# One tile per column piece of w_in, a later gate for the inputs, and a new order table

## The chip, the cores and the metric

The kernel runs on one core of one Trainium2 chip. The time is the device time of one execution in microseconds (us); the spans, waits and durations below come from one profiled execution of the kernel before the change.

## The reference

A gated linear recurrence over 768 time steps, for 4 batches and 8 heads of 48 features, gives x; a two-layer network with a leaky ReLU follows.

```python
f = 1.0 / (1.0 + np.exp(-f_logit))
for t in range(S):
    state = f[:, :, t, :, None] * state + np.einsum('bhd,bhe->bhde', k[:, :, t], v[:, :, t])
    y[:, :, t] = np.einsum('bhd,bhde->bhe', q[:, :, t], state)
x = y.transpose(0, 2, 1, 3).reshape(B * S, H * D)      # 3072 x 384
h = x @ w_in                                           # 384 x 2048
out = np.maximum(0.01 * h, h) @ w_out                  # 2048 x 384
```

## The kernel before

The time axis is cut into 6 chunks of 128 steps, and the 4 batches into 2 groups of 2. A chunk and a group make a "pair", numbered 0 to 11, and a pair has two units (batches) 0 and 1. A unit's attention is a chain over several engines:

- four loads of 192 KB each (`Lf`, `Lk`, `Lq`, `Lv`, line 98, all issued by SyncE, the engine SP);
- `gate` (two ACT instructions on f, lines 136 and 137), `cs` (TensorE sums the logs along time, lines 142 and 145), `dec` (ACT exponentials, lines 152 to 156);
- `q` and `k` (the scaling of q and k on VectorE or GpSimd, lines 167 and 161), `v` (GpSimd casts v, lines 174 and 175);
- `tq`, `tk` (transposes on TensorE, line 188), `cq`, `ck` (VectorE copies them out, line 191), `sc` (scores, line 207), `mk` (VectorE masks, line 212), `mx` (TensorE, line 240), `xt` (VectorE copies the result, x transposed, out, line 246);
- `pt`, `sf`, `sb`: the state for the next chunk (TensorE line 251, VectorE lines 256 and 257, GpSimd lines 261 and 264).

The two-layer network follows for each unit. For pairs 0 to 3 it goes unit by unit: `uu_j_a_g` (line 289) is one of four groups of 12 matmuls against a quarter of the columns of w_in, `pu` the ReLU of it on ACT (line 294). From pair 4 on, `up_j_g` (line 276) takes both units in eight groups of 6 wider matmuls, and `pr` is its ReLU (line 282). `dn_j_a_n` (line 299) is a quarter of the product with w_out, 4 matmuls; `ob` copies the result out (line 304) and `st` stores it (line 312).

The weights are cast to bf16 on the way in, by seven DMAs that GpSimd issues (`W_0` to `W_6`): w_in in three column pieces (line 111; the first and the second a quarter of the columns each, the third a half), then w_out in four pieces (line 115). All three pieces of w_in lie in one tile, `w_in_b`, 128 partitions x 3 x 2048. Group g of `uu` reads columns 512g to 512g+511, in each of the 3 slices: groups 0 and 1 read pieces 0 and 1, groups 2 and 3 read piece 2.

`hold` (`H_n`, line 128) is a tiny DMA issued by SP that reads an element of piece n of the weights, so that SP waits there until this piece has landed; what follows in SP's queue, the loads of pair 2 and later, is issued after that.

Every engine takes its instructions in the order in which a table of words, written out in the kernel, records them: `W_0_3_1_0` is a weight piece, `uu_0_1_2` the group 2 of pair 0, unit 1. Waits between engines are set by the recording layer from the tiles that instructions read and write.

Of the kernel before, what the change touches and what calls it, by code (L numbers as in the profile page):

```python
# [15 lines left out]
def kernel(  # L16
# [60 lines left out]
    w_in_b = const.tile([128, NK, FF], BF16, tag="w_in")  # L77
# [24 lines left out]
    w_in_cols = ((0, FF // 4), (FF // 4, FF // 2), (FF // 2, FF))  # L102

    def weights(piece, x, j, a):

        if (x, j, a) not in seen:
            seen.add((x, j, a))
            nc.gpsimd.tensor_copy(out=gate_w[:, 0:1], in_=raw(j, "fkqv"[x])[0:1, a, H - 1, D - 1:D])
        if piece < 3:
            lo, hi = w_in_cols[piece]  # L110
            nc.gpsimd.dma_start(out=w_in_b[:, :, lo:hi], in_=moe_w_in[:, lo:hi].rearrange("(k p) n -> p k n", p=128))  # L111
        else:
            n = NF // 4
            part = piece - 3
            nc.gpsimd.dma_start(
                out=w_out_b[:, part * n:(part + 1) * n, :],
                in_=moe_w_out[part * n * 128:(part + 1) * n * 128, :].rearrange("(p a) n -> p a n", a=n))
# [3 lines left out]
    def hold(piece):  # L121

        if piece < 3:
            hi = w_in_cols[piece][1]
            src = w_in_b[0:1, NK - 1, hi - 4:hi]
        else:
            src = w_out_b[0:1, (piece - 2) * (NF // 4) - 1, 0:4]
        nc.sync.dma_start(out=gate_s[:, 0:4], in_=src)
# [137 lines left out]
    def columns(ff):  # L266

        c, a = divmod(ff, 4)
        return slice(512 * c + a, 512 * c + 512, 4)

    def up(j, g):
        pm = st[j]["pm", g] = ps_m.tile([128, 2, 256], FP32, name="pm", tag="pm")
        for i in range(2):
            ff = 2 * g + i
            for kk in range(NK):
                nc.tensor.matmul(pm[:, i, :], w_in_b[:, kk, columns(ff)],  # L276
# [7 lines left out]
    def up_unit(j, a, g):  # L284
        pm = st[j]["pu", a, g] = ps_m.tile([128, 4, 128], FP32, name="pm", tag="pm")
        for i in range(4):
            ff = 4 * g + i
            for kk in range(NK):
                nc.tensor.matmul(pm[:, i, :], w_in_b[:, kk, columns(ff)], st[j]["xT"][:, kk, a, :],  # L289
# [58 lines left out]
    Lf_0_0 Lk_0_0 Lq_0_0 Lv_0_0 Lf_0_1 gate_0_0 Lk_0_1 Lq_0_1 cs_0_0 dec_0_0 Lv_0_1 v_0_0 Lf_1_0 q_0_0 k_0_0 tq_0_0  # L348
    gate_0_1 Lk_1_0 cq_0_0 Lq_1_0 cs_0_1 tk_0_0 dec_0_1 Lv_1_0 pt_0_0 ck_0_0 sf_0_0 v_0_1 Lf_1_1 sc_0_0 q_0_1 gate_1_0
    Lk_1_1 k_0_1 tq_0_1 mk_0_0_0 Lq_1_1 tk_0_1 mk_0_0_1 cs_1_0 Lv_1_1 cq_0_1 pt_0_1 dec_1_0 ck_0_1 mx_0_0 W_0_3_1_0  # L350
    sf_0_1 sc_0_1 W_1_3_1_0 xt_0_0 gate_1_1 W_2_3_1_0 mk_0_1_1 q_1_0 cs_1_1 W_3_3_1_0 dec_1_1 v_1_0 mk_0_1_0 tq_1_0
    k_1_0 v_1_1 q_1_1 tk_1_0 mx_0_1 cq_1_0 tq_1_1 sb_0_0 ck_1_0 xt_0_1 sc_1_0 k_1_1 W_4_3_1_0 W_5_3_1_0 cq_1_1 tk_1_1
    uu_0_0_0 mk_1_0_1 W_6_3_1_0 ck_1_1 uu_0_1_0 pu_0_0_0 mk_1_0_0 pu_0_1_0 sc_1_1 mx_1_0 uu_0_0_1 xt_1_0 uu_0_1_1
    mk_1_1_0 pu_0_0_1 mk_1_1_1 pt_1_0 pu_0_1_1 uu_1_0_0 mx_1_1 pu_1_0_0 uu_1_0_1 xt_1_1 pu_1_0_1 uu_0_0_2 uu_0_1_2
    pu_0_0_2 pt_1_1 pu_0_1_2 uu_0_1_3 uu_0_0_3 pu_0_1_3 dn_0_0_0 pu_0_0_3 uu_1_0_2 H_4 Lf_2_0 dn_0_1_0 pu_1_0_2 Lk_2_0
    uu_1_1_0 Lq_2_0 dn_0_1_1 dn_0_0_1 uu_1_0_3 dn_0_0_2 Lv_2_0 pu_1_0_3 dn_0_1_2 pu_1_1_0 Lf_2_1 dn_0_0_3 uu_1_1_1
    gate_2_0 Lk_2_1 ob_0_0 dn_0_1_3 sf_1_0 pu_1_1_1 st_0_0 uu_1_1_2 ob_0_1 cs_2_0 sf_1_1 Lq_2_1 dn_1_0_0 dec_2_0
    dn_1_1_0 v_2_0 st_0_1 uu_1_1_3 k_2_0 sb_0_1 Lv_2_1 gate_2_1 q_2_0 tk_2_0 dn_1_0_1 ck_2_0 Lf_3_0 pu_1_1_2 tq_2_0
    pt_2_0 dn_1_1_1 cq_2_0 pu_1_1_3 Lk_3_0 sf_2_0 sc_2_0 cs_2_1 Lq_3_0 mk_2_0_0 dn_1_1_2 dec_2_1 mk_2_0_1 dn_1_0_2
    Lv_3_0 mx_2_0 k_2_1 v_2_1 Lf_3_1 dn_1_0_3 xt_2_0 sb_1_0 tk_2_1 q_2_1 gate_3_0 Lk_3_1 uu_2_0_0 ck_2_1 tq_2_1  # L360
    pu_2_0_0 cs_3_0 Lq_3_1 cq_2_1 uu_2_0_1 dec_3_0 ob_1_0 sc_2_1 Lv_3_1 uu_2_0_2 mk_2_1_0 pu_2_0_1 q_3_0 st_1_0
    dn_2_0_0 k_3_0 pu_2_0_2 sb_2_0 pt_2_1 mk_2_1_1 gate_3_1 tq_3_0 Lf_4_0 tk_3_0 dn_1_1_3 sf_2_1 v_3_0 dn_2_0_1 Lk_4_0
    ck_3_0 cq_3_0 cs_3_1 sb_1_1 Lq_4_0 mx_2_1 dec_3_1 sc_3_0 xt_2_1 dn_2_0_2 Lv_4_0 v_3_1 k_3_1 uu_2_1_0 q_3_1 Lf_4_1
    ob_1_1 tk_3_1 pu_2_1_0 uu_2_1_1 mk_3_0_0 st_1_1 gate_4_0 uu_2_0_3 mk_3_0_1 pt_3_0 Lk_4_1 ck_3_1 mx_3_0 pu_2_0_3
    sf_3_0 tq_3_1 pu_2_1_1 dn_2_1_0 Lq_4_1 cq_3_1 xt_3_0 uu_2_1_2 Lv_4_1 sc_3_1 pu_2_1_2 cs_4_0 Lf_5_0 mk_3_1_1
    dn_2_1_1 dec_4_0 mk_3_1_0 uu_3_0_0 Lk_5_0 gate_4_1 mx_3_1 k_4_0 q_4_0 Lq_5_0 dn_2_1_2 xt_3_1 sb_2_1 pu_3_0_0
    cs_4_1 Lv_5_0 dn_2_0_3 dec_4_1 uu_3_1_0 ob_2_0 Lf_5_1 tk_4_0 q_4_1 pu_3_1_0 pt_3_1 uu_3_1_1 ck_4_0 st_2_0 gate_5_0
    sf_3_1 v_4_0 tq_4_0 uu_3_1_2 Lk_5_1 k_4_1 tq_4_1 cq_4_0 pu_3_1_2 pt_4_0 dn_3_1_0 Lq_5_1 sf_4_0 pu_3_1_1 cs_5_0
    tk_4_1 Lv_5_1 v_5_0 dec_5_0 uu_3_1_3 ck_4_1 cq_4_1 uu_2_1_3 sb_3_0 Lf_6_0 pu_3_1_3 sc_4_2 pu_2_1_3 Lk_6_0 uu_3_0_1
    v_4_1 mk_4_1_1 gate_5_1 dn_2_1_3 q_5_0 k_5_0 Lq_6_0 uu_3_0_2 pu_3_0_1 mk_4_0_0 sb_3_1 Lv_6_0 dn_3_1_1 mk_4_0_1  # L370
    pu_3_0_2 cs_5_1 mk_4_1_0 Lf_6_1 uu_3_0_3 dec_5_1 ob_2_1 mx_4_2 Lk_6_1 pu_3_0_3 k_5_1 q_5_1 tq_5_0 st_2_1 dn_3_1_2
    xt_4_0 v_5_1 tk_5_0 xt_4_1 dn_3_0_0 Lq_6_1 cq_5_0 tq_5_1 ck_5_0 tk_5_1 Lv_6_1 pt_4_1 dn_3_0_1 sf_4_1 Lf_7_0 up_4_0
    ck_5_1 dn_3_0_2 cq_5_1 Lk_7_0 pr_4_0 sc_5_2 gate_6_0 up_4_1 Lq_7_0 mk_5_1_0 dn_3_0_3 mk_5_0_1 Lv_7_0 pr_4_1 up_4_2
    mk_5_0_0 Lf_7_1 dn_3_1_3 mk_5_1_1 pr_4_2 up_4_3 Lk_7_1 pt_5_0 mx_5_2 pr_4_3 Lq_7_1 up_4_4 xt_5_0 Lv_7_1 cs_6_0
    sf_5_0 pr_4_4 up_4_5 ob_3_0 Lf_8_0 sb_5_0 dec_6_0 cs_6_1 up_4_6 ob_3_1 st_3_0 pt_5_1 pr_4_5 sb_4_0 dn_4_0_0 sf_5_1
    pr_4_6 up_4_7 st_3_1 xt_5_1 dec_6_1 v_6_0 dn_4_0_1 Lk_8_0 up_5_0 pr_4_7 q_6_0 Lq_8_0 dn_4_0_2 gate_7_0 up_5_1
    Lv_8_0 dn_4_0_3 k_6_0 Lf_8_1 pr_5_0 tq_6_0 ob_4_0 cs_7_0 pr_5_1 tq_6_1 Lk_8_1 up_5_2 cq_6_0 dec_7_0 sb_4_1 cq_6_1
    dn_5_0_0 st_4_0 up_5_3 pr_5_2 sb_5_1 Lq_8_1 tk_6_0 pr_5_3 cs_7_1 ck_6_0 tk_6_1 pt_6_0 dec_7_1 dn_5_0_1 v_7_0
    ck_6_1 Lv_8_1 sf_6_0 pt_6_1 up_5_4 Lf_9_0 sf_6_1 q_7_0 dn_4_1_0 pr_5_4 Lk_9_0 sc_6_2 gate_8_0 up_5_5 Lq_9_0
    mk_6_0_0 k_7_0 dn_4_1_1 mk_6_0_1 Lv_9_0 pr_5_5 up_5_6 mk_6_1_0 v_8_0 tq_7_0 Lf_9_1 mk_6_1_1 pr_5_6 tk_7_0 pt_7_0  # L380
    dn_5_0_2 ck_7_0 Lk_9_1 cq_7_0 tk_7_1 up_5_7 sf_7_0 Lq_9_1 pt_7_1 ck_7_1 tq_7_1 pr_5_7 dn_4_1_2 sf_7_1 Lv_9_1
    cs_8_0 dn_5_0_3 dec_8_0 Lf_10_0 mx_6_2 ob_5_0 gate_9_0 cq_7_1 st_5_0 dn_5_1_0 sb_6_0 xt_6_0 cs_8_1 xt_6_1 Lk_10_0
    dn_5_1_1 dec_8_1 sb_6_1 up_6_0 Lq_10_0 dn_5_1_2 pr_6_0 Lv_10_0 q_8_0 up_6_1 sc_7_2 Lf_10_1 pr_6_1 up_6_2 mk_7_0_0
# [12 lines left out]
    up_8_5 mk_10_0_0 pr_9_2 dn_9_0_0 pr_8_5 up_9_3 tk_11_1 pr_9_3 pt_9_1 up_9_4 sf_9_1 dn_9_0_1 pr_9_4 ck_11_1 sb_9_1
    up_9_5 sc_11_2 pr_9_5 v_11_0 up_9_6 mk_11_0_0 dn_9_0_2 mk_11_1_1 pr_9_6 up_9_7 mk_11_0_1 up_8_6 mk_11_1_0 pr_9_7
# [41 lines left out]
```

## Time and profile before

| | |
|---|---|
| time, median of 3 runs | 195.93 us (194.6 to 196.33) |
| time of the profiled execution | 195.9 us |
| its span (first to last instruction) | 194.1 us |
| TensorE busy | 173.9 us, 90% of the span |
| ScalarE / VectorE / GpSimd busy | 98.8 / 97.5 / 75.1 us |
| TensorE idle before line 289, waiting for w_in | 7.0 us in 2 waits, the longest 6.4 us |
| SP's wait at the hold, line 128 | 16.3 us |

Start times are counted from the start of the span. "Busy" of TensorE counts matmuls whose ends are modelled, so a busy TensorE need not be at its peak. PE is TensorE's matmul, PEld its weight load, DVE VectorE, ACT ScalarE, POOL GpSimd, SPq SyncE's queue.

### The profile page before, as it was taken

The page shows a single profiled execution, that of the slowest core. Times are in us where ns is not written, and L with a number is a line of the kernel's source. Part 1 is how long each engine was busy: PE and PEld are TensorE (multiplying, and loading weights), DVE is VectorE, ACT ScalarE, POOL GpSimd, SP SyncE. Part 2 cuts the span into 40 slices and gives each one's busy share as a digit, 9 for nine tenths or more (in the row PEclk, how much of TensorE's full clock was granted, in tenths as well). Part 3 has the DMA queues.
Part 4 walks back from the last instruction along what each step waited for, and adds up shares of the span by engine and source line. Part 5 has one row for each costly group of instructions (what it writes and reads, how often), then busy time and mean ns, then how long its engine had stood idle before and what let it go on. Part 6 is the DMA issues. An engine that isn't in the chain of part 4 may idle for free.

```text
span 194.1 us, 5638 instructions
## 1 busy us (share of the span) xinstructions
PE 173.9 (90%) x2360; PEld 138.1 (71%) x2360; DVE 97.5 (50%) x212; ACT 98.8 (51%) x201; POOL 75.1 (39%) x138
## 2 busy tenths in 40 slices
PE   0476229999999999999999999999999999999994
PEld 0343128977687888878888778877868888888663
DVE  2398503107688856966347737509737574200131
ACT  4544004726654788544976376974233544644200
POOL 8237060030439089401999373099653040000000
PEclk9999999999999999999999999999999999999999
DMA  6999999934999889979798989991001000021122
GB/s 121 210 197 169 204 195 206 173 75 111 200 213 206 191 160 230 178 171 211 162 239 195 210 184 212 194 244 57 26 19 57 28 5 3 3 78 44 41 81 81
DMA packets 106113, 27.10 MB, mean 140 GB/s; under 512 B 100456, under 2 KB 105192, under 8 KB 106088
## 3 DMA queue, kind: packets, MB, share of 16 engines
q1 hardware_dynamic: 104312, 23.60, 57.1%
q0 software_dynamic: 1776, 3.15, 9.0%
q8 instruction: 18, 0.29, 0.6%
q14 instruction: 7, 0.06, 0.1%
HBM read 25.17 MB, written 4.72 MB: 154 GB/s over the span
## 4 chain that ended last, share of the span: by engine, by line
PE 84%; DMA 8%; SPq 5%; POOL 1%; issue 0%; DVE 0%
PE po L299 31%; PE pm L276 22%; PE pm L289 12%; DMA w_in_b<-in_moe_w_in_dram 6%; PE py L240 5%; PE tp L188 5%; SPq L98 5%; PE pw L207 3%; PE cs L142 2%; DMA v_raw<-in_v_dram 2%; PE pt L251 2%; PE po L321 1%; POOL w_in_b L111 1%; PE cs L145 1%; DVE osb L327 0%
## 5 line engine op out<-in xcount | busy, mean ns | idle before, releaser
L299 PE MATMUL po<-w_out_b,gT 128*128 128x384 bf16 x368 | 71.4, 326 | 0.0
L282 ACT ACTIVATE gT<-pm 128x512 bf16<-128x512 f32 x64 | 37.9, 598 | 38.2 <-PE pm L276 37.5
L276 PE MATMUL pm<-xT,w_in_b 128*128 128x256 bf16 x384 | 51.5, 273 | 0.0
L299 PEld LDWEIGHTS <-gT 128*128 128x128 bf16 x368 | 34.1, 98 | 16.2 <-issue 0.2
L276 PEld LDWEIGHTS <-w_in_b 128*128 128x128 bf16 x384 | 40.7, 114 | 4.6
L212 DVE TENSOR_TENSOR wm<-pw,ut 128x512 bf16<-128x512 f32 x48 | 30.5, 683 | 14.8 <-PE pw L207 14.6
L289 PE MATMUL pm<-xT,w_in_b 128*128 128x128 bf16 x384 | 27.2, 225 | 7.0 <-DMA w_in_b<-in_moe_w_in_dram 7.0
L304 DVE COPY osb<-po 128x384 f32<-128x384 f32 x23 | 12.6, 553 | 37.8 <-PE po L299 36.5
L294 ACT ACTIVATE gT<-pm 128x512 bf16<-128x512 f32 x32 | 18.7, 596 | 24.8 <-PE pm L289 24.5
L289 PEld LDWEIGHTS <-w_in_b 128*128 128x128 bf16 x384 | 24.5, 116 | 9.3 <-issue 6.8
L167 POOL TENSOR_TENSOR qh<-q_raw,a_t 128x384 bf16<-128x384 f32 (+1 forms) x12 | 15.7, 1308 | 23.3 <-ACT a_end L156 15.8
L174 POOL CAST v_b<-v_raw 128x384 bf16<-128x384 f32 (+1 forms) x18 | 11.3, 625 | 33.1 <-DMA v_raw<-in_v_dram 32.3
L246 DVE CAST xT<-py 128x384 bf16<-128x384 f32 x24 | 12.7, 553 | 16.9 <-PE py L240 16.8
L152 ACT ACTIVATE em_t<-cs 128x384 bf16<-128x384 f32 x24 | 11.7, 488 | 12.3 <-PE cs L145 8.7
L261 POOL TENSOR_TENSOR sf<-sf,a_end 128x192 f32<-128x192 f32 x20 | 10.5, 523 | 18.9 <-DVE sf L257 18.6
L264 POOL CAST sb<-sf 64x192 bf16<-64x192 f32 x40 | 14.2, 354 | 5.2 <-PE py L240 2.8
L142 PE MATMUL cs<-lf,ut 128*128 128x384 bf16 x24 | 8.5, 352 | 7.5 <-ACT lf L137 7.5
L136 ACT ACTIVATE e_t<-f_raw 128x384 f32<-128x384 f32 (+1 forms) x18 | 11.3, 629 | 6.4 <-DMA f_raw<-in_f_logit_dram 6.4
L191 DVE COPY kT<-tp 128x512 bf16<-128x512 bf16 x24 | 10.1, 421 | 8.2 <-PE tp L188 8.0
L188 PE MATMUL tp<-ident,qh 128*128 128x128 bf16 x96 | 10.2, 234 | 2.3 <-DVE qh L167 2.2
L153 ACT ACTIVATE a_t<-cs 128x384 bf16<-128x384 f32 x24 | 11.7, 489 | 0.0
L137 ACT ACTIVATE lf<-e_t 128x384 bf16<-128x384 f32 (+1 forms) x18 | 11.4, 631 | 0.6
(46 smaller groups left out, 172.2 us busy)
## 6 DMA issues: line engine op xcount, KB each, us to landing
f_raw<-in_f_logit_dram SPq DMA_DIRECT2D x24, 192.0 KB, 3.8
k_raw<-in_k_dram SPq DMA_DIRECT2D x24, 192.0 KB, 3.8
q_raw<-in_q_dram SPq DMA_DIRECT2D x24, 192.0 KB, 4.0
v_raw<-in_v_dram SPq DMA_DIRECT2D x24, 192.0 KB, 3.9
out_dram<-osb SPq DMA_DIRECT2D x17, 192.0 KB, 2.9
w_out_b<-in_moe_w_out_dram POOLq DMA_DIRECT2D x4, 384.0 KB, 7.5
out_dram<-osb SPq DMA_DIRECT2D x12, 96.0 KB, 1.7
w_in_b<-in_moe_w_in_dram POOLq DMA_DIRECT2D x2, 384.0 KB, 8.1
```

The costliest lines, as they stand in the source:

```text
L142: nc.tensor.matmul(t[:, 0:H * D], ut, lf[:, a, :, 0:D], start=True, stop=True)
L167: eng.tensor_mul(qhs[j % NR][:, a, :, 0:D], raw(j, "q")[:, a], st[j]["a"][:, a].rearrange("t a (h d) -> t a h d", d=D))
L188: nc.tensor.transpose(tp[:, p, :], scaled(j, x)[:, a, 2 * p:2 * p + 2, :], ident)
L212: nc.vector.tensor_mul(wm, st[j].pop(("pw", a, i)), ut[:, None, :].to_broadcast([128, P2, 128]))
L246: nc.vector.tensor_copy(out=xT[:, :, a, :], in_=st[j].pop(("py", a))[:, 0:NK, :])
L264: nc.gpsimd.tensor_copy(out=sb[rows, a, :, i * D:i * D + D], in_=sf[rows, a])
L276: nc.tensor.matmul(pm[:, i, :], w_in_b[:, kk, columns(ff)], st[j]["xT"][:, kk].rearrange("t a s -> t (a s)"), start=(kk == 0), stop=(kk == ...
L282: nc.scalar.activation(gT[:, 2 * g:2 * g + 2, :], st[j].pop(("pm", g)), AF.Prelu, alpha=0.01)
L289: nc.tensor.matmul(pm[:, i, :], w_in_b[:, kk, columns(ff)], st[j]["xT"][:, kk, a, :], start=(kk == 0), stop=(kk == NK - 1))
L294: nc.scalar.activation(gT[:, 4 * g:4 * g + 4, 128 * a:128 * a + 128], st[j].pop(("pu", a, g)), AF.Prelu, alpha=0.01)
L299: nc.tensor.matmul(po, st[j]["g"][:, ff, 128 * a:128 * a + 128], w_out_b[:, ff, :], start=(ff == 0), stop=(ff == NF - 1))
L304: nc.vector.tensor_copy(out=osb, in_=st[j].pop(("po", a)))
```

## The change

Each column piece of w_in becomes a tile of its own, and the matmuls pick the piece and the columns in it. The hold in the order table names piece 5 (the third quarter of w_out) where it named piece 4 (the second). The order table is a new one: the same words, in another order.

```diff
-    w_in_b = const.tile([128, NK, FF], BF16, tag="w_in")
+    w_in_cols = ((0, FF // 4), (FF // 4, FF // 2), (FF // 2, FF))
+    w_in_b = [const.tile([128, NK, hi - lo], BF16, name="w_in_b", tag=f"w_in{lo}") for lo, hi in w_in_cols]
...
     def weights(piece, x, j, a):
...
-            nc.gpsimd.dma_start(out=w_in_b[:, :, lo:hi], in_=moe_w_in[:, lo:hi].rearrange("(k p) n -> p k n", p=128))
+            nc.gpsimd.dma_start(out=w_in_b[piece], in_=moe_w_in[:, lo:hi].rearrange("(k p) n -> p k n", p=128))
...
     def hold(piece):
         if piece < 3:
-            hi = w_in_cols[piece][1]
-            src = w_in_b[0:1, NK - 1, hi - 4:hi]
+            src = w_in_b[piece][0:1, NK - 1, 0:4]
...
-    def columns(ff):
+    def w_in(kk, ff):
 
         c, a = divmod(ff, 4)
-        return slice(512 * c + a, 512 * c + 512, 4)
+        piece = [hi > 512 * c for lo, hi in w_in_cols].index(True)
+        lo = 512 * c - w_in_cols[piece][0]
+        return w_in_b[piece][:, kk, lo + a:lo + 512:4]
...
-                nc.tensor.matmul(pm[:, i, :], w_in_b[:, kk, columns(ff)],
+                nc.tensor.matmul(pm[:, i, :], w_in(kk, ff),
...
-                nc.tensor.matmul(pm[:, i, :], w_in_b[:, kk, columns(ff)], st[j]["xT"][:, kk, a, :],
+                nc.tensor.matmul(pm[:, i, :], w_in(kk, ff), st[j]["xT"][:, kk, a, :],
...
-    Lk_1_1 k_0_1 tq_0_1 mk_0_0_0 Lq_1_1 tk_0_1 mk_0_0_1 cs_1_0 Lv_1_1 cq_0_1 pt_0_1 dec_1_0 ck_0_1 mx_0_0 W_0_3_1_0
-    sf_0_1 sc_0_1 W_1_3_1_0 xt_0_0 gate_1_1 W_2_3_1_0 mk_0_1_1 q_1_0 cs_1_1 W_3_3_1_0 dec_1_1 v_1_0 mk_0_1_0 tq_1_0
-    k_1_0 v_1_1 q_1_1 tk_1_0 mx_0_1 cq_1_0 tq_1_1 sb_0_0 ck_1_0 xt_0_1 sc_1_0 k_1_1 W_4_3_1_0 W_5_3_1_0 cq_1_1 tk_1_1
-    uu_0_0_0 mk_1_0_1 W_6_3_1_0 ck_1_1 uu_0_1_0 pu_0_0_0 mk_1_0_0 pu_0_1_0 sc_1_1 mx_1_0 uu_0_0_1 xt_1_0 uu_0_1_1
-    mk_1_1_0 pu_0_0_1 mk_1_1_1 pt_1_0 pu_0_1_1 uu_1_0_0 mx_1_1 pu_1_0_0 uu_1_0_1 xt_1_1 pu_1_0_1 uu_0_0_2 uu_0_1_2
-    pu_0_0_2 pt_1_1 pu_0_1_2 uu_0_1_3 uu_0_0_3 pu_0_1_3 dn_0_0_0 pu_0_0_3 uu_1_0_2 H_4 Lf_2_0 dn_0_1_0 pu_1_0_2 Lk_2_0
-    uu_1_1_0 Lq_2_0 dn_0_1_1 dn_0_0_1 uu_1_0_3 dn_0_0_2 Lv_2_0 pu_1_0_3 dn_0_1_2 pu_1_1_0 Lf_2_1 dn_0_0_3 uu_1_1_1
-    gate_2_0 Lk_2_1 ob_0_0 dn_0_1_3 sf_1_0 pu_1_1_1 st_0_0 uu_1_1_2 ob_0_1 cs_2_0 sf_1_1 Lq_2_1 dn_1_0_0 dec_2_0
...
+    Lk_1_1 k_0_1 tq_0_1 Lq_1_1 mk_0_0_0 tk_0_1 mk_0_0_1 cs_1_0 Lv_1_1 cq_0_1 pt_0_1 dec_1_0 W_0_3_1_0 ck_0_1 mx_0_0
+    W_1_3_1_0 sc_0_1 xt_0_0 gate_1_1 sf_0_1 sb_0_0 q_1_0 cs_1_1 W_2_3_1_0 k_1_0 dec_1_1 tq_1_0 mk_0_1_0 W_3_3_1_0
+    q_1_1 W_4_3_1_0 tk_1_0 mk_0_1_1 W_5_3_1_0 v_1_0 ck_1_0 mx_0_1 tq_1_1 cq_1_0 W_6_3_1_0 xt_0_1 sc_1_0 v_1_1 k_1_1
+    cq_1_1 tk_1_1 uu_0_0_0 mk_1_0_0 ck_1_1 uu_0_1_0 pu_0_0_0 mk_1_0_1 sc_1_1 pu_0_1_0 mk_1_1_0 uu_0_0_1 mx_1_0
+    pu_0_0_1 pt_1_0 xt_1_0 uu_0_1_1 mk_1_1_1 uu_1_0_0 pu_0_1_1 mx_1_1 pu_1_0_0 uu_1_0_1 xt_1_1 pt_1_1 sf_1_0 pu_1_0_1
+    uu_0_0_2 sf_1_1 uu_0_1_2 pu_0_0_2 pu_0_1_2 uu_0_1_3 uu_0_0_3 pu_0_1_3 dn_0_0_0 pu_0_0_3 uu_1_1_0 dn_0_1_0 pu_1_1_0
+    uu_1_0_2 uu_1_1_1 pu_1_0_2 H_5 Lf_2_0 dn_0_0_1 pu_1_1_1 Lk_2_0 dn_0_1_1 Lq_2_0 dn_0_0_2 Lv_2_0 uu_1_0_3 Lf_2_1
+    uu_1_1_2 gate_2_0 Lk_2_1 dn_0_1_2 dn_0_0_3 pu_1_0_3 Lq_2_1 cs_2_0 ob_0_0 dn_0_1_3 dec_2_0 Lv_2_1 dn_1_0_0 v_2_0
+    uu_1_1_3 q_2_0 st_0_0 dn_1_0_1 ob_0_1 sb_1_0 pu_1_1_3 Lf_3_0 k_2_0 tq_2_0 gate_2_1 dn_1_1_0 cq_2_0 sb_0_1 st_0_1
+    tk_2_0 pt_2_0 pu_1_1_2 dn_1_1_1 ck_2_0 Lk_3_0 sf_2_0 sb_1_1 sc_2_0 cs_2_1 mk_2_0_1 Lq_3_0 dn_1_1_2 dec_2_1 v_2_1
...
```

## The prediction

> **What bounds the kernel now.** I read the page first: the strip of slices and the chain that ended last.
>
> ```profile
> span 194.1 us, 5638 instructions
> ...
> PE   0476229999999999999999999999999999999994
> ...
> DMA  6999999934999889979798989991001000021122
> ...
> PE 84%; DMA 8%; SPq 5%; POOL 1%; issue 0%; DVE 0%
> ```
>
> TensorE is full from slice 7 (about 29 us) to the end, and 84% of the chain is its own work: 163 of 194.1 us. What is not TensorE in the chain (SPq 5%, DMA 8%, POOL 1%, 27 us) lies ahead of that, in the slices where the strip falls to 2. So only the start and the density of the rest can move the end. The windows show the start:
>
> ```profile
> 15.00:20.00 5.00, 3.29 (x41) 1.95 (x40) 4.33 (x10) 1.98 (x5) 3.03 (x6) 1.00 1.04 168
> 20.00:25.00 5.00, 0.91 (x5) 0.46 (x5) 1.95 (x5) 0.00 (x0) 0.93 (x3) 1.00 1.17 207
> 25.00:30.00 5.00, 1.96 (x19) 1.99 (x20) 0.00 (x0) 0.59 (x1) 2.57 (x6) 1.00 1.09 195
> ...
> 40.00:45.00 5.00, 5.00 (x53) 3.74 (x52) 0.22 (x1) 2.16 (x5) 1.25 (x4) 1.00 0.12 25
> ```
>
> (Columns: stretch; its length; busy us of PE, PEld, DVE, ACT, POOL with counts; granted clock; DMA share; GB/s.) From 20 to 28 us every engine is nearly idle and DMA is full; from 40 to 45 us TensorE is full and DMA idle. The timeline of TensorE names the hole:
>
> ```profile
> 20.15 0.61 PE L188 MATMUL tp<-ident,kh 128*128 128x128 bf16 x4 [0.32 <-DVE kh L161]
> 21.30 0.30 PE L289 MATMUL pm<-xT,w_in_b 128*128 128x128 bf16 x1 [0.54 <-DMA w_in_b<-in_moe_w_in_dram]
> 28.04 2.62 PE L289 MATMUL pm<-xT,w_in_b 128*128 128x128 bf16 x23 [6.44 <-DMA w_in_b<-in_moe_w_in_dram]
> ```
>
> One matmul of uu_0_0_0 runs at 21.30, the second at 28.04. Both read piece 0 of w_in, in slices 0 and 1 of the tile. The timeline of GpSimd, the chain and the tile views give the landings:
>
> ```profile
> 14.22 2.49 POOL L111 DMA_DIRECT2D w_in_b<-in_moe_w_in_dram  x3
> 16.71 0.58 POOL L115 DMA_DIRECT2D w_out_b<-in_moe_w_out_dram  x1
> ...
> 24.07 0.51 POOL L174 CAST v_b<-v_raw 128x384 bf16<-128x384 f32 x1 [6.04 <-DMA v_raw<-in_v_dram]
> ...
> 26.04 1.66 POOL L115 DMA_DIRECT2D w_out_b<-in_moe_w_out_dram  x3
> ...
> DMA to landing us min/median/max: 7.0/9.2/12.0
> ```
>
> The last line is w_in's: piece 0 lands at 14.22 + 7.0 = 21.2 us, piece 1 at 15.16 + 9.2 = 24.4, piece 2 at 15.94 + 12.0 = 27.9. The second matmul started when piece 2 was there. In one tile of 3 slices each piece is a strided column block, and the strides of all three reach across slice 1; in the instruction list before, the second weight load waits for pieces 1 and 2 at once; in the changed list the three waits stand at groups 0, 1 and 2. So the 6.44 us is a wait for data that is not read. W_out's pieces (the same view: 5.5 to 13.0 us) follow at 29.7, 31.5, 33.4 and 35.4: GpSimd's queue lands in order, one piece of 384 KB each 1.85 us.
>
> Last, SP's queue:
>
> ```profile
> 31.56 0.73 SPq L128 DMA_DIRECT2D gate_s<-w_out_b  x1
> 32.34 0.40 SPq L98 DMA_DIRECT2D f_raw<-in_f_logit_dram  x1
> ...
> 37.64 0.78 SPq L98 DMA_DIRECT2D k_raw<-in_k_dram  x1
> 45.37 0.36 SPq L312 DMA_DIRECT2D out_dram<-osb  x1
> 45.77 0.43 SPq L98 DMA_DIRECT2D q_raw<-in_q_dram  x1
> ```
>
> The hold opens at 31.56, with piece 4 (31.5). Six loads of pair 2 go out, then the store st_0_0 holds the queue from 38.4 to 45.4: the 40 to 45 us hole of DMA.
>
> **The change, part by part.** The counts of instructions on every engine stay (2360 matmuls); so it is waits and order alone.
>
> *The three tiles: −6.44 us.* TensorE goes on at 21.3 instead of 28.04, if each later piece is there in time. I walk the new order:
> - uu_0_0_0 and uu_0_1_0: 24 matmuls. After the pause 23 took 2.62 us, 114 ns each, and later 12 take 0.67 us, 56 each, though the granted clock reads 1.00 in every window. The slow start, 24 x 58 ns = 1.4 us, is paid once in both kernels: 0. If waits brought it back it is +1.4.
> - sc_1_1, 0.54: 21.3 + 2.7 + 0.54 = 24.5. Then uu_0_0_1 needs piece 1 (24.4): 0, at most +0.7 if the first groups run fast.
> - uu_0_0_1, mx_1_0, pt_1_0, uu_0_1_1, uu_1_0_0, mx_1_1, uu_1_0_1, pt_1_1: four groups of 0.67, two mx of 0.4 to 0.5, two pt of 0.17, 3.9 us: 28.4. Then uu_0_0_2 needs piece 2 (27.9). I take 0.
>
> *GpSimd's queue.* W_2 now stands behind sb_0_0 (0.51 + 0.74 = 1.25 us), so it is issued at about 17.2 instead of 15.94. Piece 1 is still in flight until 24.4 and the pieces go one after another, so the landing stays at 27.9; without that cover it is +1.25. W_4 to W_6 are issued by 21 instead of 26 to 27.7, with no gain, as the queue of transfers was never empty. The cast v_1_0 moves behind W_5: 17.3 becomes about 19.8; its reader mx_1_0 comes at 25, so 5 us to spare. v_1_1 still waits for its load, landed at 24.0.
>
> *The later hold: +0.3.* Piece 5 instead of 4: 33.4 − 31.5 = 1.86 us later. Behind it in SP's queue stand all loads of pair 2 and later; f goes out at 33.4 + 0.73 = 34.2. The first load of the kernel took 3.1 us to land (0.74 to 3.82 by its DMA records); before, beside two weight pieces, f took 3.8. So 37.3 to 38.0; two ACT steps of 0.52 put cs_2_0 at 38.4 to 39.1. TensorE arrives there at: 28.4 + 15 groups in all less the 6 done, 9 x 0.67, + 7 dn x 0.65 = 39.0. W_out's pieces are needed at 31 (29.7), 34.6 (31.5), 36 (33.4) and 38.5 (35.4): all there. So it meets TensorE with nothing to spare; I take +0.3, bounds 0 and 1.86.
>
> *The rest of the order: 0.* Before, cs_2_0 ran at 46.57 with one dn more done (0.65): TensorE is 46.57 − 39.0 − 0.65 = 6.9 us earlier at the same work. It keeps that if pair 3's loads come as much earlier: before, Lf_3_0 went out at 47.56, after the store's hold; now Lq_2_1 and Lv_2_1 stand ahead of st_0_0, whose osb is copied after dn_0_0_3, at about 40, and Lf_3_0 follows at 40.5, 7 us earlier. As to density: 92 groups of dn at 0.65, 64 of up at 0.65, 31 of uu at 0.67, 20 units of attention at 1.6 (cs 0.27, two transposes 0.45, pt 0.17, sc 0.28, mx 0.45), 1.7 left of pairs 0 and 1, 1.4 of slow start and the last 2.65 (line 321) make 160 us of the 163.3 after 28.04. About 3 us are small pauses; a new order can win or lose of them: 0, bounds −1.5 and +1.5.
>
> Sum: −6.44 + 0.3 = −6.1; span 188.0. Around the span lie 195.9 − 194.1 = 1.8 us: **189.8 us**. The profiled execution (195.9) is at the median (195.93).
>
> **The rivals.**
>
> *Piece 2 or the casts late.* GpSimd now issues seven pieces in a row, while VectorE is at 4.33 of 5 us busy (15 to 20 us); before, three of them went out with VectorE at 0.00 (25 to 30). Against: the piece issued at 16.71 took 0.58, those at 26.04 1.66 / 3 = 0.55. If each of the four issues from W_2 on waited half a VectorE step (0.68 / 2, the wm row), with W_2's 1.25 it comes to 2.6; should the transfers follow, piece 2 lands at 30.5, TensorE waits 2.1 at uu_0_0_2, and may turn slow again (1.4): 191.9 to 193.3. The Trainium skill's page "SBUF — State Buffer" ("SBUF: two separate sides") says that GpSimd can't write the descriptors of its DMAs while VectorE runs an operation in a two-port mode; by it this rival would be the case, but the 0.58 beside 0.55 bears out almost none of it.
>
> *The loads decide: no change.* The v_raw of pair 1 was issued at 14.17 and landed at 24.0, 9.8 us, as it ran beside w_in; the median is 3.9. If f of pair 2, beside the last piece of w_out, were as slow, it lands at 44.0, cs_2_0 runs at 45, 6 us of the 6.4 are back: 195.5. Against: only one piece (1.9 us) is then left in that queue.
>
> *Slower: the hold and the stores chain up.* The place is SP's queue. Ahead of pair 3's k, q and v loads now stands st_0_1, whose copy ob_0_1 follows q_2_0 on VectorE, which needs f_2_0. If f_2_0 lands late, as above, ob_0_1, st_0_1 and pair 3's loads are late with it, and TensorE, through with pairs 0 and 1, stands twice: 6 us at cs_2_0 and, as the store's hold before lasted 7.0, some 4 at cs_3_0 after the work between: 199.5. It decides from f landing after 44.4 (38.0 + 6.4).
>
> *The matmuls still wait for the whole of w_in.* Then only the hold and the order act: 196. The separate waits in the instruction list speak against it.
>
> **How the numbers follow.** Forecast 0.72 (own range 188.3 to 191.3: the sum with −1.5 and +1.5); late pieces 0.13 (192 to 193.3); no change 0.07; slower 0.06; still one wait 0.02. 1% of 195.93 is about what measurement can tell: under 193.97 is faster, over 197.89 slower. Faster 0.72 + 0.13 − 0.01, same 0.07 + 0.02 + 0.01, slower 0.06. The range reaches into the late pieces, 193.2, and down to 187.8 for a denser rest and the spread of the runs (194.6 to 196.33); the other cases above it hold under 0.2.
>
> **What would show it.** Right: TensorE at line 290 (289 before) from 21.3 on, waits for w_in under 1 us together; pieces landing at 21.2, 24.4, 27.9; SP's hold near 33.4; cs of pair 2 at 39 to 40; DMA no longer idle from 40 to 45. Wrong: a wait of over 2 us at uu_0_0_2 (late pieces), before cs_2_0 (late f), or many new small pauses after 50 us, with the last matmul of line 322 ending after 188.

## The result, and the profile after

The changed kernel takes 189.33 us (median of 5, 188.66 to 194.24), the kernel before in the same comparison 196.07 (median of 5, 194.6 to 196.37): a ratio of 0.966 [0.9612, 0.9707], the brackets being the 95% interval. The forecast was 189.8. Executions over 1.5% longer than the fastest of their kernel are left out of all ratios, here the one at 194.24 (mean granted clock 0.991). The profiled execution took 189.33, with a span of 187.5; the prediction's sum for the span had come to 188.0.

The page of the changed kernel, its strip of slices (tenths busy) and its chain:

```profile
span 187.5 us, 5631 instructions
...
PE   0575899999999999999999999999999999999994
...
DMA  6999999499997998998998999971110100111122
...
PE 87%; DMA 6%; SPq 3%; issue 2%; POOL 1%; DVE 0%; POOLq 0%
```

The slices of 2 before TensorE fills up are gone. TensorE's own share of the chain is 87% of 187.5 = 163 us, as before (84% of 194.1 = 163): its work did not change, and the whole difference lies in what is not TensorE.

The timeline of TensorE, the changed kernel (start, busy us of the group; in brackets the idle time ahead of it and what ended it):

```profile
20.26 0.61 PE L187 MATMUL tp<-ident,kh 128*128 128x128 bf16 x4
...
21.34 2.75 PE L290 MATMUL pm<-xT,w_in_b 128*128 128x128 bf16 x24 [0.48 <-DMA w_in_b<-in_moe_w_in_dram]
...
24.57 0.91 PE L290 MATMUL pm<-xT,w_in_b 128*128 128x128 bf16 x12
...
28.56 3.02 PE L290 MATMUL pm<-xT,w_in_b 128*128 128x128 bf16 x48
```

The 24 matmuls of `uu_0_0_0` and `uu_0_1_0` run through from 21.34. The 6.44 us behind the first of them are gone, and neither `uu_0_0_1` (24.57) nor `uu_0_0_2` (28.56) has a wait for w_in ahead of it.

The timelines of GpSimd and of SP (the queues' issues), the changed kernel:

```profile
14.12 1.72 POOL L111 DMA_DIRECT2D w_in_b<-in_moe_w_in_dram  x2
...
17.35 0.80 POOL L111 DMA_DIRECT2D w_in_b<-in_moe_w_in_dram  x1
18.15 1.65 POOL L115 DMA_DIRECT2D w_out_b<-in_moe_w_out_dram  x3
...
20.75 0.53 POOL L115 DMA_DIRECT2D w_out_b<-in_moe_w_out_dram  x1
```

```profile
33.60 0.74 SPq L127 DMA_DIRECT2D gate_s<-w_out_b  x1
34.38 0.40 SPq L99 DMA_DIRECT2D f_raw<-in_f_logit_dram  x1
...
41.66 0.62 SPq L313 DMA_DIRECT2D out_dram<-osb  x1
42.33 0.43 SPq L99 DMA_DIRECT2D f_raw<-in_f_logit_dram  x1
```

By their DMA records the pieces land at 21.30, 23.52, 27.30 (w_in) and 29.14, 30.94, 33.58, 35.43 (w_out). The hold opens at 33.60 with piece 5, and `Lf_3_0` goes out at 42.33 (47.56 before). The windows, the changed kernel (columns as above):

```profile
20.00:25.00 5.00, 4.41 (x47) 3.61 (x44) 2.40 (x6) 1.19 (x2) 2.02 (x5) 1.00 1.18 213
25.00:30.00 5.00, 5.00 (x109) 4.58 (x107) 3.38 (x8) 2.95 (x5) 0.00 (x0) 1.00 1.08 212
30.00:35.00 5.00, 4.99 (x72) 4.37 (x70) 0.00 (x0) 3.08 (x7) 0.00 (x0) 1.00 0.58 113
...
40.00:45.00 5.00, 5.00 (x58) 3.43 (x57) 3.58 (x9) 2.72 (x7) 4.13 (x10) 1.00 1.03 225
```

TensorE is full from 25 us. DMA's hole at 40 to 45 us is filled (1.03 for 0.12); a smaller one has come at 30 to 35 (0.58), where SP stands at the hold until 33.60 and the last of GpSimd's pieces are under way.

One subtraction shows that this is all of it. From the second matmul of `uu_0_0_0`, the first that ran on without a break, to the end, the kernel before took 194.1 − 28.04 = 166.1 us. In the changed kernel the group starts at 21.34 and its second matmul 115 ns later (2.75 us / 24): 187.5 − 21.45 = 166.0. The rest of the kernel is as long as it was; it begins 6.6 us earlier. This remainder, from the start of the unbroken group to the end of the span, is used for the experiments too (for the changed kernel 187.5 − 21.34 = 166.2).

### The profile page after: what moved, and what is told of

Its sections match the earlier page's. It is cut to its first block, busy times and chain, and to the rows that moved or that the text cites. A ratio compares the mean times of both kernels' runs of the same rounds, so it can differ in the third digit from the quotient of the medians.

```text
span 187.5 us, 5631 instructions
## 1 busy us (share of the span) xinstructions
PE 173.9 (93%) x2360; PEld 137.9 (74%) x2360; DVE 98.3 (52%) x212; ACT 99.1 (53%) x201; POOL 76.0 (41%) x138
## 4 chain that ended last, share of the span: by engine, by line
PE 87%; DMA 6%; SPq 3%; issue 2%; POOL 1%; DVE 0%; POOLq 0%
PE po L300 32%; PE pm L277 23%; PE pm L290 13%; PE py L239 5%; PE tp L187 5%; DMA w_in_b<-in_moe_w_in_dram 4%; PE pw L206 3%; SPq L99 3%; DMA v_raw<-in_v_dram 2%; PE cs L141 2%; PE pt L250 2%; PE po L322 1%; PE cs L144 1%; POOL v_b L173 0%; POOL v L174 0%
## 5 line engine op out<-in xcount | busy, mean ns | idle before, releaser
L173 POOL CAST v_b<-v_raw 128x384 bf16<-128x384 f32 (+1 forms) x18 | 12.4, 690 | 25.7 <-DMA v_raw<-in_v_dram 25.4
L190 DVE COPY qT<-tp 128x512 bf16<-128x512 bf16 x24 | 10.1, 419 | 7.3 <-PE tp L187 7.0
L160 POOL TENSOR_TENSOR kh<-k_raw,em_t 128x768 bf16<-128x768 f32 x6 | 9.9, 1647 | 7.7 <-issue 7.6
```

Of the source, the lines that this page charges most:

```text
L190: nc.vector.tensor_copy(out=turned(j, x)[:, P2 * a:P2 * a + P2, :], in_=st[j].pop(("tp" + x, a)))
```

## The experiments

The kernels ran in three groups, each on one chip beside runs of the kernel before: the first four, the next four, the last four. In the first two expectations theory A is the prediction's own: the gain is the false wait for w_in and nothing else. The later ones say themselves what their theories are.

### The three tiles alone

The kernel before with the tiles of the change, and with the order table and the hold (`H_4`) of before.

```diff
-    w_in_b = const.tile([128, NK, FF], BF16, tag="w_in")
+    w_in_b = [const.tile([128, NK, hi - lo], BF16, name="w_in_b", tag=f"w_in{lo}") for lo, hi in w_in_cols]
...
```

> Three tiles, but the order table and the hold (piece 4) of the kernel before. Theory A (the whole gain is the false wait for the pieces of w_in; order and hold bring nothing by themselves): TensorE goes on at 21.3, waits for w_in under 1 us together, time 189 to 190.3, as the changed kernel. Theory B (the new order is needed to keep the gain, since here Lq_2_1 and Lv_2_1 stand behind the store st_0_0 and pair 2 starves an earlier TensorE): the start is as early, but 2 to 4 us are lost between cs_2_0 and 60 us, time 191.5 to 194.

Measured: 188.78 us (188.65 to 190.57), ratio 0.9662 [0.961, 0.9714]. Its timeline of TensorE:

```profile
21.27 2.56 PE L290 MATMUL pm<-xT,w_in_b 128*128 128x128 bf16 x24 [0.49 <-DMA w_in_b<-in_moe_w_in_dram]
```

This one edit brings the whole gain. The old order loses nothing either: its store `st_0_0`, which held SP's queue until 45.37 before, goes out at 38.97, as the copy that it stores comes earlier with everything else.

### The order table alone

The kernel before, one tile, with the new table and `H_5`.

```diff
-    sf_0_1 sc_0_1 W_1_3_1_0 xt_0_0 gate_1_1 W_2_3_1_0 mk_0_1_1 q_1_0 cs_1_1 W_3_3_1_0 dec_1_1 v_1_0 mk_0_1_0 tq_1_0
+    W_1_3_1_0 sc_0_1 xt_0_0 gate_1_1 sf_0_1 sb_0_0 q_1_0 cs_1_1 W_2_3_1_0 k_1_0 dec_1_1 tq_1_0 mk_0_1_0 W_3_3_1_0
...
```

> One tile for w_in as before, but the new order table with the hold at piece 5. Theory A: the wait at the second matmul of uu_0_0_0 is back (6.4 us, until piece 2 at 27.3 to 27.9) and the time is that of the kernel before within 1 us: 195 to 197. Theory B (the order is worth something of its own, 1 to 3 us, by earlier GpSimd work, no store ahead of Lq_2_1 and a denser rest): 193 to 195.

Measured: 196.04 us (194.62 to 196.63), ratio 0.9991 [0.9965, 1.0018]. The wait is back, between the same two matmuls (timeline of TensorE):

```profile
21.89 0.29 PE L289 MATMUL pm<-xT,w_in_b 128*128 128x128 bf16 x1 [0.80 <-DMA w_in_b<-in_moe_w_in_dram]
28.07 2.62 PE L289 MATMUL pm<-xT,w_in_b 128*128 128x128 bf16 x23 [5.88 <-DMA w_in_b<-in_moe_w_in_dram]
```

The order, with its hold at piece 5, is worth nothing that can be measured: alone its interval reaches from 0.7 us faster to 0.4 us slower, and beside the tiles (the run before this one) the two ratios, 0.9662 and 0.966, differ by less than their intervals, about 1 us to either side.

### One tile, its pieces laid out one after another

The kernel before, with its one tile and its table, but each piece in a contiguous stretch of the tile's columns instead of in strided blocks. This asks whether it was the one tile or the reach of the strides that made the wait.

```diff
-            nc.gpsimd.dma_start(out=w_in_b[:, :, lo:hi], in_=...)
+            nc.gpsimd.dma_start(out=w_in_b[:, NK * lo:NK * hi].rearrange("p (k n) -> p k n", k=NK), in_=...)
...
-                nc.tensor.matmul(pm[:, i, :], w_in_b[:, kk, columns(ff)],
+                nc.tensor.matmul(pm[:, i, :], w_in(kk, ff),   # NK * lo + kk * (hi - lo) + 512 * c - lo + a, step 4
```

> One tile for w_in, but laid out piece after piece (each piece's 3 slices contiguous), with the order table and the hold of the kernel before. If the false wait came from the address ranges of strided pieces that reach across each other (A), the pieces are apart now and the time is that of the tiles alone, 189 to 190.3, with waits at groups 0, 1 and 2. If a tile is waited for as a whole (C), the 6.4 us wait stays and the time is 195 to 197.

Measured: 190.28 us (188.78 to 190.43), ratio 0.9701 [0.9654, 0.9747]. Its timeline of TensorE:

```profile
22.29 2.75 PE L292 MATMUL pm<-xT,w_in_b 128*128 128x128 bf16 x24 [1.95 <-DMA w_in_b<-in_moe_w_in_dram]
```

One tile is enough when the pieces don't reach across each other: all 24 matmuls run on from 22.29, when piece 0 alone is there (landed 22.24). So the false wait came from the strides. This kernel's remainder is 188.5 − 22.29 = 166.2 us. Its span is 1.6 us above that of the tiles alone (186.9), 1.0 of it a later landing of piece 0 in that execution (22.24 for 21.22). Whether this layout makes it later isn't settled: the intervals overlap.

### The hold, earlier, later and away

The changed kernel, its table with `H_4`, with `H_6`, and with no hold word.

```diff
-    uu_1_0_2 uu_1_1_1 pu_1_0_2 H_5 Lf_2_0 dn_0_0_1 pu_1_1_1 Lk_2_0 dn_0_1_1 Lq_2_0 dn_0_0_2 Lv_2_0 uu_1_0_3 Lf_2_1
+    uu_1_0_2 uu_1_1_1 pu_1_0_2 H_4 Lf_2_0 ...   (first kernel)
+    uu_1_0_2 uu_1_1_1 pu_1_0_2 H_6 Lf_2_0 ...   (second)
+    uu_1_0_2 uu_1_1_1 pu_1_0_2 Lf_2_0 ...       (third)
```

With `H_4`:

> The changed kernel with the hold at piece 4 instead of 5: pair 2's loads go out 1.9 us earlier, at about 32, beside two pieces of w_out instead of one. By my sum the later hold costs 0.3 (bounds 0 and 1.86), so this gives 189.0 to 189.4 (up to 0.3 faster than the changed kernel). If TensorE really had nothing to spare at cs_2_0, 188 to 188.5. If the hold at 5 is worth something because it keeps the loads from delaying w_out's last pieces (needed by dn_0_0_2 at 35.3 and dn_0_0_3 at 38.7), it is 0.5 to 1 us slower than the changed kernel.

With `H_6`:

> The changed kernel with the hold at piece 6, the last of w_out: pair 2's loads go out 1.85 us later still, near 35.5. By my walk there is nothing to spare at cs_2_0, so all of it would be lost: 191.2. The trace of the changed kernel speaks for 1.0 us to spare (the gate's second step ends at 38.3, cs_2_0 runs at 39.33), so that 0.8 us is lost at cs_2_0 and the time is 190.1 (189.7 to 190.5). If the loads of pair 2 have much more slack than either says, 189.3 as the changed kernel.

Without a hold:

> The changed kernel without the hold: pair 2's loads go out from 15 us on and run beside the weights. Theory A (the weights' queue keeps most of the rate, as v_raw of pair 1 took 6.7 to 9.8 us beside it): pieces land up to 15% later, piece 2 at 28 to 29.5, TensorE waits 0.3 to 1.5 us for w_in, pair 2 is there early, time 189.3 to 191. Theory B (the two queues share by halves): piece 0 at 22.5 to 23.5, piece 2 at 31 to 33, the waits for w_in come back by 3 to 5 us, time 192.5 to 195.

| kernel | time, us | ratio | remainder, us |
|---|---|---|---|
| `H_4` | 189.44 (187.91 to 189.79) | 0.966 [0.9611, 0.9709] | 188.0 − 21.86 = 166.1 |
| `H_6` | 189.32 (188.37 to 192.8) | 0.9675 [0.963, 0.9719] | 187.9 − 20.47 = 167.4 |
| no hold | 189.04 (188.46 to 189.17) | 0.9688 [0.9658, 0.9719] | 186.7 − 20.30 = 166.4 |

Of these three only the hold at piece 6 reaches TensorE, in `cs_2_0` (timeline of TensorE, `H_6`):

```profile
39.73 0.32 PE L141 MATMUL cs<-lf,ut 128*128 128x384 bf16 x1 [0.96 <-ACT lf L136]
```

There it costs 0.96 us in the trace, and the remainder lies 1.0 to 1.3 above the other two; the times don't tell the three apart. The changed kernel itself, with the hold at piece 5, had no such wait in its first profile, and one of 0.46 us when it ran again on the third chip (same view of that run):

```profile
39.88 0.32 PE L141 MATMUL cs<-lf,ut 128*128 128x384 bf16 x1 [0.46 <-ACT lf L136]
```

In the times a hold at piece 5 costs nothing measurable against one at 4, and its absence brings nothing measurable either. Without it f of pair 2 goes out at 14.08 and takes 11.0 us beside the weights; these land later, piece 2 at 27.60 and piece 6 at 36.18 (26.18 and 33.83 with `H_6` on the same chip), but TensorE waits for none of them.

### Piece 2 of w_in late

The changed kernel with `W_2` issued behind `W_3` and `W_4`: the first rival, made to happen.

```diff
-    ... q_1_0 cs_1_1 W_2_3_1_0 k_1_0 dec_1_1 tq_1_0 mk_0_1_0 W_3_3_1_0
-    q_1_1 W_4_3_1_0 tk_1_0 ...
+    ... q_1_0 cs_1_1 k_1_0 dec_1_1 tq_1_0 mk_0_1_0 W_3_3_1_0
+    q_1_1 W_4_3_1_0 W_2_3_1_0 tk_1_0 ...
```

> The changed kernel with piece 2 of w_in issued behind two pieces of w_out, so that it lands some 3.7 us later, near 31.2. It tests my rival of late pieces and its price. TensorE comes to uu_0_0_2 at 28.5, so it waits 2.5 to 2.9 us; the time is 189.3 + 2.7 = 192.0 (191.7 to 192.5) if the wait alone counts, 193 to 193.5 if TensorE turns slow again for 24 matmuls after it. If the walk of the new order was wrong and there is slack behind, under 191.5.

Measured: 191.26 us (190.71 to 192.07), ratio 0.9812 [0.9771, 0.9852]. Piece 2 landed at 30.08. The timelines of TensorE and GpSimd of this kernel:

```profile
30.13 3.05 PE L290 MATMUL pm<-xT,w_in_b 128*128 128x128 bf16 x48 [2.85 <-DMA w_in_b<-in_moe_w_in_dram]
```

```profile
17.19 1.15 POOL L115 DMA_DIRECT2D w_out_b<-in_moe_w_out_dram  x2
18.33 0.77 POOL L111 DMA_DIRECT2D w_in_b<-in_moe_w_in_dram  x1
```

A late piece is paid nearly in full: the remainder is 189.1 − 20.31 = 168.8 us, 2.6 above the changed kernel's 166.2, for a wait of 2.85; against it, less of the slow start was paid in this execution (the first 24 matmuls took 2.21 us, not 2.75). The median lies 1.9 to 2.2 us above those of `H_6` and of no hold on the same chip, and a little under the expected 191.7 to 192.5, on a chip where the kernel before too was faster (194.84). The slow turn that the rival added on top (1.4 us) didn't come: the 48 matmuls behind the wait take 3.05 us, and 3.02 in the changed kernel.

### A warm TensorE

The walk paid 24 x 58 ns for a slow start. The changed kernel with 8 matmuls of 384 columns that nobody reads, in the gaps ahead of `cs_1_1` (4), `mx_0_1` (2) and `uu_0_0_0` (2).

```diff
+    def warm(n):
+        po = ps_o.tile([128, KD], FP32, name="po", tag="po")
+        for _ in range(n):
+            nc.tensor.matmul(po, ident, warm_s, start=True, stop=True)
...
-    ... q_1_0 cs_1_1 W_2_3_1_0 ... v_1_0 ck_1_0 mx_0_1 ... cq_1_1 tk_1_1 uu_0_0_0 ...
+    ... q_1_0 wu_4 cs_1_1 W_2_3_1_0 ... v_1_0 ck_1_0 wu_2 mx_0_1 ... cq_1_1 tk_1_1 wu_2 uu_0_0_0 ...
```

> The changed kernel with eight more matmuls (128x384, nobody reads them) put where TensorE stands between 14.5 and 21.3: four before cs_1_1, two before mx_0_1, two before uu_0_0_0, each 0.32 us at the slow rate. It tests the term 'slow start, 1.4 us, paid once'. If TensorE needs steady work to reach 56 ns per matmul of 128 columns, the first 24 of line uu take about 1.35 instead of 2.75 us. Theory A (then the landing of pieces 1 and 2 is the next limit): new waits before uu_0_0_1 (piece 1 at 23.5 to 24.4) and uu_0_0_2 (piece 2 at 27.3 to 27.9) take most of it back, time 188.5 to 189.2, 0.2 to 0.8 under the changed kernel. Theory B (the slow start is on the path by itself): 1.4 faster, 187.9. If the extra matmuls do not change the rate, or delay pair 1's attention, 189.3 to 190.5.

Measured: 188.04 us (187.64 to 188.34), ratio 0.9642 [0.9611, 0.9673], beside 0.9688 [0.9658, 0.9719] for the kernel without a hold and 0.9675 for `H_6` on the same chip (the changed kernel itself did not run on it). Its timeline of TensorE:

```profile
20.40 1.50 PE L297 MATMUL pm<-xT,w_in_b 128*128 128x128 bf16 x24
...
22.95 0.86 PE L297 MATMUL pm<-xT,w_in_b 128*128 128x128 bf16 x12 [0.72 <-DMA w_in_b<-in_moe_w_in_dram]
```

The 24 matmuls take 1.50 us instead of 2.77 (the kernel without a hold), 1.27 less; 0.72 of that goes into a new wait for piece 1, so some 0.6 is left. That the slow start is real and can be taken away is shown; its size goes by the execution (the 24 matmuls took 2.21 to 2.77 us in the eight traces without extra matmuls in which they run through). As for the gain, it was tried again on a third chip, with the changed kernel beside it.

> The changed kernel itself, unaltered, beside the next two on one chip, so that differences under 1 us can be read: ratio to before 0.966 (0.961 to 0.971), as first measured.

> The changed kernel with the eight extra matmuls again, beside the changed kernel on one chip. Its first trace showed the 24 matmuls at 1.50 instead of 2.77 us and a new wait of 0.72 us for piece 1. Theory A (landing of the pieces takes about half of the 1.3 back): 0.5 to 0.9 us under the changed kernel, ratio to before 0.961 to 0.964. Theory B (all of it is gained): 1.3 us under, ratio 0.959. Nothing gained: equal ratios.

Measured: the changed kernel 189.57 us (189.09 to 189.84), ratio 0.9688 [0.9659, 0.9718]; with the extra matmuls 190.02 (189.26 to 194.56), ratio 0.9713 [0.9677, 0.9749]. The gain did not come again. The 24 matmuls took 1.50 us there too, but the mean granted clock was 0.982 to 0.991 in five of its seven executions, and 0.999 to 1.0 in all of the changed kernel beside it. In the profiled one of the five (192.77 us) ACT stood 3.82 us for a load of f that landed at 98.35, TensorE stood 2.55 us behind ACT, and its rate fell; the lines are in the last section. Whether the other four lost theirs in the same way, and whether the extra matmuls have to do with it, is open.

### Two attempts at a faster version

More extra matmuls, from `cs_0_0` on (28 in all), with `mx_1_0` and `pt_1_0` ahead of `uu_0_0_1`, to speed up the attention of pairs 0 and 1 and cover the wait for piece 1:

```diff
-    Lf_0_0 Lk_0_0 Lq_0_0 Lv_0_0 Lf_0_1 gate_0_0 Lk_0_1 Lq_0_1 cs_0_0 dec_0_0 ...
+    Lf_0_0 Lk_0_0 Lq_0_0 Lv_0_0 Lf_0_1 gate_0_0 Lk_0_1 Lq_0_1 wu_8 cs_0_0 dec_0_0 ...   (then wu_5, wu_4, wu_6, wu_3, wu_2)
...
-    ... mk_1_1_0 uu_0_0_1 mx_1_0 pu_0_0_1 pt_1_0 xt_1_0 uu_0_1_1 ...
+    ... mk_1_1_0 mx_1_0 pt_1_0 xt_1_0 uu_0_0_1 pu_0_0_1 uu_0_1_1 ...
```

> A candidate for a faster version: extra matmuls also ahead of cs_0_0 (8), tq_0_0 (5) and tq_0_1 (4), six instead of four before cs_1_1 and three before mx_0_1, so that the attention of pairs 0 and 1 too may run at the fast rate; and uu_0_0_1 moved behind mx_1_0 and pt_1_0, so that the wait for piece 1 is filled. If the landing of piece 0 at 20 to 21.3 and of piece 2 at 26.2 to 27.9 are the limits, the faster attention brings nothing before piece 0 and the filled wait up to 0.5: 0.2 to 0.6 us under the kernel with eight extra matmuls. If the early matmuls delay cs_0_0 or tq_0_0, up to 1 us over it.

Measured: 190.62 us (188.77 to 193.23), ratio 0.9722 [0.9678, 0.9767]: no gain. `uu_0_0_0` starts at 21.51, after a wait of 0.16 us that piece 0 ended, so in that execution a faster attention could not have brought it earlier; the weights are let go when the v of pair 1, unit 0, has landed. The attention wasn't fast throughout either: the clock record has full rate from 7.14 to 13.97 us and half rate from there to 20.80.

So the last kernel lets the weights go one load earlier, at q of pair 1 instead of v, with the 8 extra matmuls:

```diff
-    ... dec_1_0 W_0_3_1_0 ck_0_1 mx_0_0 W_1_3_1_0 ...
+    ... dec_1_0 W_0_2_1_0 ck_0_1 mx_0_0 W_1_2_1_0 ...   (W_2 to W_6 likewise)
```

> The kernel with the eight extra matmuls, and the weights let go when q of pair 1's first unit has landed (near 13.1) instead of v (near 14.0). If the landing of the pieces is the limit, all pieces land 0.8 us earlier and the time is 0.3 to 0.8 under the kernel with the eight matmuls alone. Against it: k, q and v of pair 1's second unit run beside the weights' queue, which takes most of the rate; q_raw and k_raw may land 1 to 3 us later and with them tq_1_1 and tk_1_1, which stand ahead of uu_0_0_0 on TensorE: then uu_0_0_0 starts 0.5 to 2 us later and the time is as much over it.

Measured: 195.49 us (191.05 to 197.24, at mean granted clocks of 0.972 to 1.0), ratio 0.9773 [0.9728, 0.9819]. Letting the weights go earlier is worse: the shortest of its executions is longer than the longest of the changed kernel on the same chip (189.84). In its trace `uu_0_0_0` started at 23.89, where it had started at 20.40 and 21.31 with the same extra matmuls. The reason is a load that came late. The q_raw of pair 1, unit 1, issued at 13.19 beside the first weight piece, landed at 19.95, 6.8 us later (3.7 in the changed kernel's profile), and VectorE stood for it (timeline of VectorE, this kernel):

```profile
20.04 0.56 DVE L173 TENSOR_TENSOR qh<-q_raw,a_t 128x384 bf16<-128x384 f32 x1 [2.58 <-DMA q_raw<-in_q_dram]
```

The mask `mk_0_1_1` is next on VectorE, and TensorE waits 2.31 us for it ahead of `mx_0_1`, with the transposes of pair 1 and `uu_0_0_0` behind it. The v_raw behind that q_raw took 13.5 us, from 14.15 to 27.67. No kernel here clearly beats the changed one.

## Why the prediction was right

*The three tiles, −6.44.* Held. 6.6 us of the span went: the 6.44, 0.06 of the wait at the first matmul, and 0.1 in the rest. The sum had −6.1; the 0.5 between them is mostly the 0.3 of the hold, which was not paid in this execution. The tiles alone bring the ratio of the whole change.

*The slow start, 0.* Held: 24 matmuls in 2.75 us, 115 ns each, paid once as before. That the two profiles agree so well is in part luck, as the 24 took 2.21 and 2.56 us in two others.

*Pieces 1 and 2 there in time, 0 and 0.* Held, with `uu_0_0_1` at 24.57 (24.5 in the walk) and `uu_0_0_2` at 28.56 (28.4). Piece 1 is close, as the bound of +0.7 said: the changed kernel waited 0.44 us for it in the profile of the third chip. Piece 2 landed at 27.30 with 1.26 us to spare, although issued 1.4 us later than before, so the cover named (the pieces ahead of it still in flight) was there. The run with piece 2 late shows what its loss would have cost: the wait, without the slow turn.

*GpSimd's issues beside a busy VectorE.* The rival priced each issue from `W_2` on half a VectorE step longer. They took 0.80 us, 1.65 / 3 = 0.55 and 0.53, the first four of them in a stretch where VectorE was busy 4.45 of 5 us (15 to 20 us). The rule of the Trainium skill's page "SBUF — State Buffer" ("SBUF: two separate sides") that spoke for the rival shows no sign here: 0.55 beside a busy VectorE, and 0.55 beside an idle one in the kernel before. The page speaks of VectorE operations in a two-port mode, and no view here tells whether one of these was, so the rule itself is not tested. The rival's price also counted too much: `W_2` is the first of its four issues, and the three behind it can't make piece 2 late.

*The later hold, +0.3.* Right in size, wrong in one reading. The walk had `cs_2_0` with nothing to spare: lf there at 38.4 to 39.1, TensorE at 39.0. The profile has 39.33 for TensorE and, for lf (timeline of ACT, the changed kernel), 38.3:

```profile
37.21 0.53 ACT L135 ACTIVATE e_t<-f_raw 128x384 f32<-128x384 f32 x1 [1.67 <-DMA f_raw<-in_f_logit_dram]
37.77 0.53 ACT L136 ACTIVATE lf<-e_t 128x384 bf16<-128x384 f32 x1
```

So 1.0 us was to spare: f landed 2.8 us after its issue, where the walk allowed 3.1 to 3.8. In the profile of the third chip the same load took 4.2 us (34.48 to about 38.7), and `cs_2_0` waited 0.46. The term is 0 to 0.5 by execution; one piece later still, it is 0.96.

*The rest of the order, 0 with ±1.5.* Held: the order table alone is 0.9991 [0.9965, 1.0018]. Three readings under this step were off without effect. The 163.3 us "after 28.04" are TensorE's busy time there, of 166.1 in all; so the 3 us that the groups leave over are not pauses. The pauses are 166.1 − 163.3 = 2.8 us, about the same by chance, and in the changed kernel, after 21.45, they are 2.8 again. `Lf_3_0` went out at 42.33, not 40.5: what holds SP's queue now is not the store but SP's own issuing of eight loads, from 34.38 to 41.56, single ones up to 1.60 us. And the v_raw of pair 1, which the text left at 24.0, landed at 20.69.

*The rivals.* That the loads decide, and that hold and stores chain up, both needed an f of pair 2 as slow as the 9.8 us of v_raw; it took 2.8, and 4.2 on the third chip. That the matmuls still wait for all of w_in is excluded by the 24 matmuls that run through from 21.34.

## What to carry to other kernels

Where the first instruction of a group runs and the second waits, look at what each reads, and at which landing ends the wait: a landing of data that neither reads is a false dependence, from pieces whose address ranges reach across each other, and it goes with separate tiles or with a contiguous layout. Such a wait at the head of a kernel whose bounding engine is full from there on is worth its whole length, as long as each later piece is there when its reader comes; take the remainder, span less the start of the full stretch, to see whether anything was given back (here it moved by some 0.5 us with how much of the slow start fell into it: 165.6 for the tiles alone, 166.2 for the changed kernel). An order table and a gate that come along with such a change are to be run alone before they are given a part of the gain.

## What the runs showed of the hardware

The slow start isn't in the page. The strip and the windows give a granted clock of 1.00 from 20 to 25 us, while matmuls of 128 columns follow each other at 115 ns and later at 63 (3.02 us / 48). The trace's own clock record begins with a turn to full rate, at 31.55 us in the kernel before and at 24.73 in the changed one: 3.5 and 3.4 us after TensorE's unbroken stretch begins. In the other runs without extra matmuls it comes 1.5 (`W_2` late) to 4.6 us (order alone) after that. With the eight extra matmuls it comes at 15.5. The Trainium skill's page "TensorE: Matmul & The Clock Gate" (Part 1, on the clock gate) states half rate until some 3.4 us of sustained work, in a window that runs freely; turns that come sooner or later after the work begins, here 1.5 to 4.6 us, agree with it.

A pause of TensorE is not priced by its length alone. After 2.85 us (piece 2 late) the rate stayed full. In one execution with the extra matmuls, after 2.55 us (timeline of TensorE), it did not:

```profile
97.27 0.81 PE L307 MATMUL po<-w_out_b,gT 128*128 128x384 bf16 x4
100.63 0.82 PE L284 MATMUL pm<-xT,w_in_b 128*128 128x256 bf16 x6 [2.55 <-ACT gT L290]
...
102.09 1.48 PE L307 MATMUL po<-w_out_b,gT 128*128 128x384 bf16 x4
```

The same four matmuls take 1.48 us for 0.81, and the clock record has half rate from 101.3 for 3.41 us. The clock records bear on the difference. Each stretch of full or half rate that ends within its record lasts a multiple of 3.41 us (3.41, 6.83, 85.33, 163.84, 167.25 and 170.67). Counted in steps of 3.41 us from the first turn of each record, the pause of 2.55 us lies inside one step (97.90 to 101.32, TensorE busy 25% of it), and half rate begins where the step ends. The pause of 2.85 us falls on the border of two steps (busy 61% and 55%). With the weights let go earlier, a pause of 2.31 us inside one step (18.58 to 21.99, busy 31%) is followed by half rate as well. So these three cases go by the idle time inside a step, not by the length of the pause; no run was made to place a pause. Where the limit lies is not shown: the rate stayed full after a step that was busy 66% (eight extra matmuls, third chip) and fell after one of 67% (28 extra matmuls).

A load on SP's queue can be much slower beside GpSimd's weight pieces. One of 192 KB took 9.8 us (before), 11.0 (no hold) and 13.5 (weights let go earlier), against medians of 3.8 to 4.0 for such loads on the changed kernel's page. It need not be: the load that took 9.8 us before took 6.7 in the first profile of the changed kernel and 3.7 with `H_4`. What decides the share of the two queues isn't shown.
